# Edits to the opening and the ending of a convolution kernel: warm-up, order of the transposes, one operand made by VectorE, release of the weight loads, and the last tile's second half on ScalarE

## Chip, cores, metric

One NeuronCore of one Trainium2 chip. The metric is device microseconds of one execution. A profile's span is 1.8 us shorter than the time of the execution that it was taken from.

## The reference, cut to what matters

```python
B, T, D, K = 2, 4000, 512, 5          # bf16
xp = jnp.pad(x, ((0,0),(2,2),(0,0)))
h = sum(xp[:, i:i+T, :] @ w1[i] for i in range(5))   # convolution of 5 taps
h = gelu(h)[:, ::2, :]                               # stride 2
f = gelu(conv5(h, w2))[:, ::2, :]                    # the same again, stride 2
j = tanh((f @ w_f)[:, :, None] + (g @ w_g)[:, None]) # U = 8
return j @ w_o                                       # (2, 1000, 8, 512)
```

(`sum` and `conv5` stand for the loops of the original.)

## The kernel before

x is kept transposed (channels on partitions) and split into four phases, the time index modulo 4. Four products of a tap weight with a phase can be saved by making combined operands, called a0, a1, a2, a3, b1, b2, b3 (a0 is phase 2 one step back, minus phase 2). The very first tile, t0 (254 columns), must start before any of this is ready. So half of its output blocks are computed directly, tap by tap (`direct(i)`: 16 matmuls with tap i), and the other half from the combined operands (`filt("a0")`: 8 matmuls with tap 0, and so on). The second tile, t1, and all later ones use the combined operands alone.

The opening, in the program's order:

```python
NWARM = 8
memset(zero[:])                        # on POOL
...
act(warm[0:1], warm[1:2], ACT.Gelu_apprx_tanh)
xr_in = [load_xr(rt) for rt in range(2)]          # two blocks of x, 512 KB each, not transposed

def load_w1(i, after=None):
    o = load_w("sp", w1_sb[i], ...)               # tap i: 512 KB
    if after is not None:
        o.deps[("dma", after.idx)] = True         # issued only when `after` has landed

load_w1(0)
for i in (1, 3, 4, 2):
    load_w1(i, xr_in[1])
for ph in (2, 3, 1, 0):
    load_x(0, ph, 272, 528)                       # transposing DMA: the rest of x
...
warm_mm(NWARM)                                    # the warm-up: matmuls on zeros
for rt in range(2):                               # block of x
    for pp in range(2):                           # 0: even phases, 1: odd phases
        ...                                       # 8 transposes on PE, then a copy out of PSUM:
        if pp: act(o, pv, ACT.Copy)               # odd phases by ScalarE
        else:  ... tensor_copy                    # even phases by VectorE
    warm_mm(1 + rt)
...
for w in ("a0", "b1", "a3"):
    t0.shift(w)                                   # ScalarE copies a phase, moved by one column
for w in ("a1", "a2", "b3", "a0", "b1", "a3"):
    t0.xf(w)                                      # VectorE adds or subtracts
...
for i in (0, 1, 3):
    direct(i)
filt("a0", "b1")
direct(4)
filt("b3", "a3")
direct(2)
...
for w in ("a0", "b1", "a3"):
    t1.shift(w)                                   # a3 waits for the last phase of x
...
filt("b2", "a1", "a2")
for m in (0, 1):
    t0.gelu(m, ps.pair(m * NT, 256, NA))          # ScalarE; frees PSUM banks 0 and 1, where t1 starts
```

All loads are issued by SyncE, in order. A release that has not come holds every load behind it as well: in the profile of before SyncE waited 3.2 us for the second block of x and issued no load between 1.63 and 5.30. The ending evicts the last tile in two halves, both on VectorE, and stores both from SyncE.

Of the kernel before, what the change touches and what calls it, by code (L numbers as in the profile page):

```python
# [201 lines left out]
def bass_standalone__seq2seq_rnn_t_joint__speech_kernel(  # L202
# [30 lines left out]
    NSLOT = 12  # L233
    BU = B * U
    NT = 512
    NWARM = 8

    with ExitStack() as es:  # L238
        cur = [16512]

        def at(name, shape, dtype, offset=None):
            o = cur[0] if offset is None else offset
            b = Buf(nc, name, shape, dtype, o)
            if offset is None:
                cur[0] = (b.end + 31) // 32 * 32
            return b
# [21 lines left out]
        zero = at("zero", [NT], BF16)  # L268
# [11 lines left out]
        pl = Plan(nc)  # L280
        sub, add = ALU.subtract, ALU.add

        def memset(v):
            pl.op("pool", lambda e: e.memset(v.ap, 0.0), (), (v,))

        def tt(eng, o, a, b, op):
            pl.op(eng, lambda e: e.tensor_tensor(out=o.ap, in0=a.ap, in1=b.ap, op=op), (a, b), (o,))  # L287

        def act(o, i, func, scale=1.0, bias=None):
            rd = (i,) if bias is None else (i, bias)  # L290
            pl.op("act", lambda e: e.activation(o.ap, i.ap, func, scale=scale,  # L291
                                                bias=0.0 if bias is None else bias.ap), rd, (o,))

        def mm(o, pairs, start, stop, check=True):

            def fn(e):
                for n, (l, r) in enumerate(pairs):
                    ins = e.matmul(o.ap, lhsT=l.ap, rhs=r.ap, start=start and n == 0,  # L298
                                   stop=stop and n == len(pairs) - 1, skip_group_check=not check)
                return ins  # L300
            pl.op("pe", fn, [v for pr in pairs for v in pr], (o,))


        memset(zero[:])
        memset(warm[:])
        idv = ident[:]
        pl.op("pool", lambda e: e.affine_select(
# [7 lines left out]
        def load_w(eng, dst, src):  # L315
            return pl.dma(eng, lambda e: e.dma_start(dst.ap, src), (), (dst,))

        def load_xr(rt):
            dst = xr[rt][:].map(lambda a: a.rearrange("p r k c -> p (r k c)"))
            src = x[0, 4 * P * rt:4 * P * (rt + 1), :].rearrange("(p r) c -> p (r c)", r=4)  # L320
            return pl.dma("sp", lambda e: e.dma_start(dst.ap, src), (), (dst,))  # L321

        def load_x(s, ph, lo, hi):
# [5 lines left out]
            src = x[b, 4 * i0 + ph:4 * (i0 + hi - lo - 1) + ph + 1:4, :]  # L329
            pl.dma("sp", lambda e: e.dma_start_transpose(out=dst.ap, in_=src), (), (dst,))  # L330

        act(warm[0:1], warm[1:2], ACT.Gelu_apprx_tanh)
        xr_in = [load_xr(rt) for rt in range(2)]

        def load_w1(i, after=None):
            o = load_w("sp", w1_sb[i], w1[i].rearrange("(k c) d -> c k d", c=P))
            if after is not None:
                o.deps[("dma", after.idx)] = True

        load_w1(0)  # L340
        for i in (1, 3, 4, 2):
            load_w1(i, xr_in[1])
        for ph in (2, 3, 1, 0):
            load_x(0, ph, 272, 528)
        for ph in (2, 3, 1, 0):
# [4 lines left out]
        def warm_mm(n):  # L350
            o, z, zz = ps.cols(3 * NT, NT), zero[0:P], zero[:]
            for _ in range(n):
                mm(o, [(z, zz)], True, True)

        warm_mm(NWARM)
        psb = ps.h[:, :].bitcast(BF16)
        for rt in range(2):
            for pp in range(2):
                bk = 4 + 2 * pp + rt
                pv = View(psb[:, bk * 1024:(bk + 1) * 1024].rearrange("p (r k c) -> p r k c", r=2, k=NK), np.array([bk]), True)  # L360

                def fn(e, rt=rt, pp=pp, pv=pv):
                    for r in range(2):
                        for k in range(NK):
                            ins = e.transpose(pv.ap[:, r, k, :], xr[rt].h[:, 2 * r + pp, k, :], ident.h[:, :])
                    return ins
                pl.op("pe", fn, (xr[rt][:], ident[:]), (pv,))
                o = xs[0][pp::2, :, 16 + rt * P:16 + (rt + 1) * P]
                if pp:
                    act(o, pv, ACT.Copy)  # L370
                else:
                    pl.op("dve", lambda e, o=o, pv=pv: e.tensor_copy(out=o.ap, in_=pv.ap), (pv,), (o,))
            warm_mm(1 + rt)


        def shift(src, off, dst, c0, n, which):
# [4 lines left out]
        def xf(src, off, dst, c0, n, which, keep=False):  # L381


            ph = lambda r: src[r, :, off:off + n]
            o = lambda kind: dst[kind, :, c0:c0 + n]
            h = NT // 2
            if which == "b3" and keep:
                tt("dve", dst[0, :, h:h + n], ph(3), ph(1), sub)
            elif which == "a2" and keep:
                tt("dve", dst[1, :, h:h + n], ph(2), ph(0), sub)  # L390
            elif which == "a0":
                tt("dve", o(0), o(0), ph(2), sub)
            elif which == "a3":
                tt("dve", o(2), o(2), ph(0), sub)
            elif which == "b1":
                tt("dve", o(3), o(3), ph(1), sub)
            elif which == "b3":
                tt("dve", ph(3), ph(3), ph(1), sub)
            elif which == "a1":
                tt("dve", o(1), ph(0), ph(2), add)  # L400
            elif which == "a2":
                tt("dve", ph(2), ph(2), ph(0), sub)
# [141 lines left out]
        def direct(i):  # L544
            for m in (0, 1):
                for s in range(2):
                    r, d = tap_at[i][s]
                    mm(ps.cols(m * NT + 256 * s, NA),
                       [(w1_sb[i, k, m * P:(m + 1) * P], xs[0][r, k, 16 + d:16 + d + NA]) for k in range(NK)],
                       i == 0 and s == 0, i == 2, False)  # L550
# [3 lines left out]
        def filt(*which):  # L554
            for w in which:
                for m, A in base0.items():
                    C = A + NT
                    o = {"a0": A, "b1": A, "b3": A + 256, "a3": A + 256, "b2": C, "a1": C, "a2": C + 256}[w]
                    t0.product(w, m, o, w in ("a0", "b2"))

        for w in ("a0", "b1", "a3"):
            t0.shift(w)
        for w in ("a1", "a2", "b3", "a0", "b1", "a3"):
            t0.xf(w)
        wsum13(w1_sb, w1_t, "dve")
        w1sums(1, "s")
        for i in (0, 1, 3):
            direct(i)
        filt("a0", "b1")
        direct(4)  # L570
        filt("b3", "a3")
        direct(2)
# [61 lines left out]
        def tanh(v, k):  # L634

            b, u = v // U, v % U
            lo, hi = v * T2, (v + 1) * T2
            while lo < hi:
                n = min(hi - lo, RING - lo % RING)
                t = lo - v * T2  # L640
                act(jT[k, lo % RING:lo % RING + n], feT[b][k, t:t + n], ACT.Tanh,
                    bias=geT[k * BU + v:k * BU + v + 1])
                lo += n
# [36 lines left out]
        slot_sem = [[nc.alloc_semaphore(f"s_o{i}"), 0] for i in range(NSLOT)]  # L680
        pend = []
        for jt in range(ntile):
            if jt == 4:
                fe(1)
            c0 = jt * P
            while not pend and done < B * U and done * T2 < c0 + P + 900:
                pend = [(done, k) for k in range(NK)]
                done += 1
            while pend and pend[0][0] * T2 < c0 + P:
                tanh(*pend.pop(0))  # L690
            if pend:
                tanh(*pend.pop(0))
            r0, s = c0 % RING, jt % NSLOT
            last = jt == ntile - 1
            for h in range(2 if last else 1):
                w = NT // 2 if last else NT
                cl = slice(h * w, (h + 1) * w)
                v = ps.cols(bank(), w)
                mm(v, [(jT[k, r0:r0 + P], wo_sb[k, cl]) for k in range(NK)], True, True)
                o = ost[s][cl]  # L700
                if jt % 6 == 5 and not last:
                    act(o, v, ACT.Copy)
                else:
                    pl.op("dve", lambda e, o=o, v=v: e.tensor_copy(out=o.ap, in_=v.ap), (v,), (o,))  # L704
                lo = c0
                while lo < c0 + P:
                    vv = lo // T2
                    n = min((vv + 1) * T2, c0 + P) - lo
                    b, u, t = vv // U, vv % U, lo % T2
                    src = ost[s].rows(lo - c0, lo - c0 + n, cl)  # L710
                    dst = out[b, t:t + n, u, cl]
                    pl.dma("sp", lambda e, src=src, dst=dst: e.dma_start(dst, src.ap), (src,), (), slot_sem[s])
                    lo += n

        pl.emit(block, [(s[0], s[1]) for s in slot_sem])
# [28 lines left out]
```

## Time and profile before

| | before |
|---|---|
| time, median of the 3 runs | 279.28 us (279.26 to 279.63) |
| time of the profiled execution | 280.62 us |
| its span | 278.8 us |
| PE busy | 273.8 us (98%) |

From the page of the kernel before: the span, the first lines of the busy times, and the chain that ended last (the work followed back from the last instruction; shares of the span).

```profile
span 278.8 us, 3866 instructions
...
PE 273.8 (98%) x1435; PEld 138.8 (50%) x1435; DVE 188.1 (67%) x243; ACT 163.2 (59%) x193; POOL 30.9 (11%) x39
...
PE acc L298 95%; DMA w_sb<-in_w_dram 2%; DMA xr_64<-in_x_dram 1%; DVE ost_85 L704 0%; SPq L321 0%; DVEq L238 0%; DVE ost_84 L704 0%
```

The same chain in order of time, kernel before (start, length in us, what):

```profile
1.17 4.11 DMA xr_64<-in_x_dram
5.28 0.02 issue
5.30 5.44 DMA w_sb<-in_w_dram
10.74 0.05 issue
10.78 264.00 PE acc L298 x1368
274.78 0.02 issue
```

The second block of x lands at 5.28; that releases the tap-1 weights, which land at 10.74; from there PE works for 264.00 us without a break. The timeline of PE, kernel before (start, length, what; in brackets the idle time ahead and what ended it):

```profile
1.30 3.59 PE L298 MATMUL acc<-zero 128*128 128x512 bf16 x8 [1.30 <-POOL warm L284]
4.68 1.91 PE L365 MATMUL acc<-ident,xr_63 128*128 128x128 bf16 x16
6.39 0.63 PE L298 MATMUL acc<-zero 128*128 128x512 bf16 x1
6.82 1.11 PE L365 MATMUL acc<-ident,xr_64 128*128 128x128 bf16 x16
7.76 0.59 PE L298 MATMUL acc<-zero 128*128 128x512 bf16 x2
8.31 1.90 PE L298 MATMUL acc<-xs_49,w_sb 128*128 128x254 bf16 x16
10.78 3.65 PE L298 MATMUL acc<-xs_49,w_sb 128*128 128x254 bf16 x32 [0.57 <-DMA w_sb<-in_w_dram]
```

Warm-ups, transposes of the two blocks (16 in 1.7 us, one every 107 ns, then 16 in 0.9, one every 56 ns behind the first: by the trace's clock record the clock turned full at 6.92, as the second block began), fillers, `direct(0)` from 8.31. Then 0.57 us of idle time until tap 1 lands; `direct(1)` and `direct(3)` follow in one piece. This is the only place where PE waits after 1.3 us.

### The profile page before, as it was taken

How to read it: one execution, taken by the hardware profiler on the slowest of the kernel's cores; microseconds unless marked ns; L12 is line 12 of the kernel's file. 1: busy time of each engine (PE TensorE's matmuls, PEld its weight loads, DVE VectorE, ACT ScalarE, POOL GpSimd, SP SyncE). 2: the span in 40 equal slices, each digit the busy share in tenths (PEclk: the TensorE clock that was granted, in tenths of full speed). 3: DMA queues.
4: the chain of work that ended last, by engine and by line, in shares of the span. 5: the costliest groups of instructions: out<-in, count | busy, mean ns of one | idle time of the engine just before them, and what ended most of it. 6: DMA issues, size and time to landing. Idle time of an engine off the chain costs nothing.

```text
span 278.8 us, 3866 instructions
## 1 busy us (share of the span) xinstructions
PE 273.8 (98%) x1435; PEld 138.8 (50%) x1435; DVE 188.1 (67%) x243; ACT 163.2 (59%) x193; POOL 30.9 (11%) x39
## 2 busy tenths in 40 slices
PE   8999999999999999999999999999999999999995
PEld 4799954444444444444444444444444444444442
DVE  0899979866997676685434364776665766766764
ACT  2659738338327633822346475948957957966930
POOL 1000000079995000000000000000000000000000
PEclk9999999999999999999999999999999999999999
DMA  6999999992000000000000020444444445444444
GB/s 232 308 158 228 206 207 172 286 314 84 0 0 0 2 0 0 0 2 0 0 2 0 1 75 21 151 151 153 153 153 160 149 145 168 144 153 155 145 150 139
DMA packets 54719, 31.85 MB, mean 114 GB/s; under 512 B 31646, under 2 KB 54446, under 8 KB 54702
## 3 DMA queue, kind: packets, MB, share of 16 engines
q1 hardware_dynamic: 54702, 31.62, 42.4%
q8 instruction: 11, 0.18, 0.3%
q14 instruction: 6, 0.05, 0.1%
HBM read 7.86 MB, written 16.38 MB: 87 GB/s over the span
## 4 chain that ended last, share of the span: by engine, by line
PE 95%; DMA 3%; issue 0%; DVE 0%; SPq 0%; DVEq 0%
PE acc L298 95%; DMA w_sb<-in_w_dram 2%; DMA xr_64<-in_x_dram 1%; DVE ost_85 L704 0%; SPq L321 0%; DVEq L238 0%; DVE ost_84 L704 0%
## 5 line engine op out<-in xcount | busy, mean ns | idle before, releaser
L298 PE MATMUL acc<-wo_sb,jT 128*128 128x512 bf16 (+1 forms) x504 | 108.3, 377 | 0.0
L298 PEld LDWEIGHTS acc<-wo_sb,jT 128*128 128x128 bf16 x504 | 49.3, 98 | 58.8
L298 PE MATMUL acc<-xt_55,w_sb 128*128 128x500 bf16 (+1 forms) x192 | 42.1, 357 | 0.0
L291 ACT ACTIVATE jT<-feT_79,geT 128x1000 bf16<-128x1000 f32 (+6 forms) x44 | 35.8, 889 | 0.0
L291 ACT ACTIVATE jT<-feT_78,geT 128x1000 bf16<-128x1000 f32 (+4 forms) x40 | 35.1, 948 | 0.0
L298 PE MATMUL acc<-xt_54,w_sb 128*128 128x500 bf16 (+1 forms) x160 | 33.2, 342 | 0.0
L298 PEld LDWEIGHTS acc<-xt_55,w_sb 128*128 128x128 bf16 x192 | 18.8, 98 | 18.2
L291 ACT ACTIVATE cs_65<-acc 128x500 f32<-128x500 f32 (+2 forms) x13 | 7.0, 539 | 32.2 <-PE acc L298 32.2
L298 PEld LDWEIGHTS acc<-xt_54,w_sb 128*128 128x128 bf16 x160 | 15.6, 98 | 13.1
L291 ACT ACTIVATE cs_66<-acc 128x500 f32<-128x500 f32 (+2 forms) x13 | 7.0, 537 | 22.5 <-PE acc L298 22.5
L298 PE MATMUL acc<-xs_49,w_sb 128*128 128x254 bf16 (+2 forms) x112 | 15.7, 286 | 0.6 <-DMA w_sb<-in_w_dram 0.6
L291 ACT ACTIVATE ost_92<-acc 128x512 bf16<-128x512 f32 x10 | 6.0, 597 | 16.4 <-PE acc L298 16.4
L704 DVE CAST ost_81<-acc 128x512 bf16<-128x512 f32 x11 | 7.6, 691 | 10.4 <-PE acc L298 10.4
L704 DVE CAST ost_87<-acc 128x512 bf16<-128x512 f32 x10 | 6.9, 692 | 10.3 <-PE acc L298 10.3
L298 PE MATMUL acc<-xs_49,w_t 128*128 128x246 bf16 (+2 forms) x72 | 13.8, 315 | 0.0
L287 DVE TENSOR_TENSOR ty_68<-ty_68,acc 128x1000 f32<-128x1000 f32 (+2 forms) x9 | 9.7, 1077 | 5.2 <-PE acc L298 5.2
L287 DVE TENSOR_TENSOR ty_67<-ty_67,acc 128x1000 f32<-128x1000 f32 (+2 forms) x9 | 9.7, 1077 | 5.1 <-PE acc L298 5.1
L298 PEld LDWEIGHTS acc<-xs_49,w_sb 128*128 128x128 bf16 x112 | 10.7, 97 | 4.1 <-DMA w_sb<-in_w_dram 0.8
L291 ACT ACTIVATE ost_86<-acc 128x512 bf16<-128x512 f32 x10 | 5.9, 593 | 11.4 <-PE acc L298 11.4
L287 DVE TENSOR_TENSOR ty_69<-ty_69,acc 128x1000 f32<-128x1000 f32 (+1 forms) x8 | 8.5, 1061 | 3.5 <-PE acc L298 3.3
L298 PE MATMUL acc<-xt_55,w_t 128*128 128x500 bf16 (+1 forms) x48 | 10.0, 340 | 0.0
L704 DVE CAST ost_85<-acc 128x512 bf16<-128x512 f32 (+1 forms) x12 | 7.7, 646 | 2.6 <-PE acc L298 2.6
(113 smaller groups left out, 368.4 us busy)
## 6 DMA issues: line engine op xcount, KB each, us to landing
w_sb<-in_w_dram SPq DMA_DIRECT2D x10, 512.0 KB, 6.7
out_dram<-ost_81 SPq DMA_DIRECT2D x11, 128.0 KB, 1.9
out_dram<-ost_83 SPq DMA_DIRECT2D x10, 128.0 KB, 1.9
out_dram<-ost_85 SPq DMA_DIRECT2D x10, 128.0 KB, 1.9
out_dram<-ost_89 SPq DMA_DIRECT2D x10, 128.0 KB, 1.9
out_dram<-ost_82 SPq DMA_DIRECT2D x9, 128.0 KB
out_dram<-ost_84 SPq DMA_DIRECT2D x9, 128.0 KB
out_dram<-ost_86 SPq DMA_DIRECT2D x9, 128.0 KB
```

The source lines that it names most:

```text
L287: pl.op(eng, lambda e: e.tensor_tensor(out=o.ap, in0=a.ap, in1=b.ap, op=op), (a, b), (o,))
L291: pl.op("act", lambda e: e.activation(o.ap, i.ap, func, scale=scale, bias=0.0 if bias is None else bias.ap), rd, (o,))
L298: ins = e.matmul(o.ap, lhsT=l.ap, rhs=r.ap, start=start and n == 0, stop=stop and n == len(pairs) - 1, skip_group_check=not check)
L704: pl.op("dve", lambda e, o=o, v=v: e.tensor_copy(out=o.ap, in_=v.ap), (v,), (o,))
```

## The change

The intent: fill PE's wait for tap 1 with work that needs tap 0 alone. a0 needs only the even phases, so these are turned first, VectorE makes a0 in one subtraction from the phase itself (read one column back, so not aligned to 4 bytes) without ScalarE's copy, and its products go right behind `direct(0)`. A longer warm-up without fillers, started earlier by a zero fill on VectorE instead of POOL, is meant to have the clock full before the transposes, which in the profile of before began 2.2 us ahead of the turn (4.69 and 6.92). The release of tap 3 is moved from the landing of the second x block to that of tap 0 (tap 4 and tap 2 stand behind it in the same queue), so that until then only tap 1 is queued behind tap 0. The second half of the last tile goes to ScalarE and its queue. The core of the diff, with cuts:

```diff
-    NWARM = 8
+    NWARM = 10
...
-        memset(zero[:])
+        pl.op("dve", lambda e: e.memset(zv.ap, 0.0), (), (zv,))
...
-        load_w1(0)
-        for i in (1, 3, 4, 2):
-            load_w1(i, xr_in[1])
+        came.append(load_w1(0))          # came = [x block 0, x block 1, tap 0]
+        for i, after in ((1, came[1]), (3, came[2]), (4, None), (2, None)):
+            load_w1(i, after)
...
-        for rt in range(2):
-            for pp in range(2):
+        for pp in range(2):
+            for rt in range(2):
...
-            warm_mm(1 + rt)
...
+            if which == "a0" and keep:
+                tt("dve", o(0), src[2, :, off - 1:off - 1 + n], ph(2), sub)
...
-        for w in ("a0", "b1", "a3"):
+        for w in ("b1", "a3"):
             t0.shift(w)
-        for w in ("a1", "a2", "b3", "a0", "b1", "a3"):
+        for w in ("a0", "a1", "a2", "b3", "b1", "a3"):
             t0.xf(w)
...
-        for i in (0, 1, 3):
-            direct(i)
-        filt("a0", "b1")
+        direct(0)
+        filt("a0")
+        direct(1)
+        direct(3)
+        filt("b1")
...
-                if jt % 6 == 5 and not last:
+                if h == 1 or jt % 6 == 5 and not last:
...
-                    pl.dma("sp", lambda e, ...
+                    pl.dma(("sp", "act")[h], lambda e, ...
```

More of the change, by code (lines that the diff above doesn't have):

```diff
@@ L301, in mm @@
             pl.op("pe", fn, [v for pr in pairs for v in pr], (o,))
-        memset(zero[:])
+        zv = zero[:]
+        pl.op("dve", lambda e: e.memset(zv.ap, 0.0), (), (zv,))
         memset(warm[:])
@@ L330, in load_x @@
             pl.dma("sp", lambda e: e.dma_start_transpose(out=dst.ap, in_=src), (), (dst,))
+        came = [load_xr(rt) for rt in range(2)]
         act(warm[0:1], warm[1:2], ACT.Gelu_apprx_tanh)
-        xr_in = [load_xr(rt) for rt in range(2)]
         def load_w1(i, after=None):
@@ L338, in load_w1 @@
                 o.deps[("dma", after.idx)] = True
-        load_w1(0)
-        for i in (1, 3, 4, 2):
-            load_w1(i, xr_in[1])
+            return o
+        came.append(load_w1(0))
+        for i, after in ((1, came[1]), (3, came[2]), (4, None), (2, None)):
+            load_w1(i, after)
         for ph in (2, 3, 1, 0):
@@ L386, in xf @@
             h = NT // 2
-            if which == "b3" and keep:
+            if which == "a0" and keep:
+                tt("dve", o(0), src[2, :, off - 1:off - 1 + n], ph(2), sub)
+            elif which == "b3" and keep:
                 tt("dve", dst[0, :, h:h + n], ph(3), ph(1), sub)
@@ L711, in bass_standalone__seq2seq_rnn_t_joint__speech_kernel @@
                     dst = out[b, t:t + n, u, cl]
-                    pl.dma("sp", lambda e, src=src, dst=dst: e.dma_start(dst, src.ap), (src,), (), slot_sem[s])
+                    pl.dma(("sp", "act")[h], lambda e, src=src, dst=dst: e.dma_start(dst, src.ap), (src,), (), slot_sem[s])
                     lo += n
```

## The prediction

> **What bounds it now.** TensorE. PE is busy 273.8 of 278.8 us (page), and the chain of waits is one PE piece from 10.78 to 274.78. So only the first 10.8 us and the last 4 can give time. The chain of the opening: load of the second x block (lands 5.29) -> its landing releases the issue of the tap-1 weights (5.30) -> these land at 10.74 -> PE. Before that, the timeline shows 8 warm-ups at 427 ns from 1.30, 16 transposes at 107 ns (4.69 to 6.39), then the second block at 56 ns: the granted clock went full at 6.92. Tap 0 runs 8.31 to 10.05; PE then waits 0.6 us for tap 1. The tail: the last two half evictions share VectorE (0.41 us each), their two stores share one queue (issues end 276.34 and 276.83, last landing 278.10), then 0.7 us of closing.
>
> **What the change moves.**
> - Zero fill on VectorE instead of POOL (0.53 us): warm-up starts about 0.3 us earlier, at 1.0; ten warm-ups then end near 5.25, where the second block is there (5.29).
> - Even phases first: 16 transposes, then the second VectorE copy ends near 7.9 if the clock turns at 6.9 as before (7.1 if it turns by 5). Tap 0 starts at 7.7 to 8.0 (tap-0 weights land 7.62).
> - Operand a0 is one VectorE subtraction, no ScalarE copy (1.04 us).[...] I expect 0.69 us as for aligned ones[...].
> - Its 8 products (109 ns each = 0.87 us) run behind tap 0 and fill PE's wait for tap 1: the main gain.
> - Tap-3 weights now wait for tap 0's landing (7.6 instead of 5.72). Tap 1 then lands earlier (estimate 9.3 to 10.5), tap 3 near 12.5 (before 12.41[...]), and the x phases behind it 0.3 to 0.6 later.
>
> **On the critical path.** Tap 1 starts near 10.6 with a0 done: 1.1 us ahead of before. Some is lost: tap 3 may be waited for; the second tile cannot start before the first tile's gelu (21.97 to 22.56), which stands on ScalarE behind the copy of the last x phase (landed 21.02). That caps the gain at 23.81 - 22.60 = 1.2 us less the delay of that phase. Head: 0.75 us gained. Tail: the second half goes to ScalarE and its queue, about 0.25 us.
>
> **Predicted: 278.3 us, range 277.6 to 279.1.** Faster by over 2%: 1%; within 2%: 98%; slower: 1%.
>
> **What would show it.** Right: one PE block from about 7.9, a0 products directly behind tap 0; PE's last matmul 0.7 earlier; last landing 0.25 nearer to it. Wrong: PE waits for tap-3 weights over 0.5 us; a0 over 1.2 us and PE waiting on VectorE; a PE gap near 22 to 24 on gelu or late x phases.
>
> **What would make it wrong.** The clock turning late:[...] before turned 2.2 us after transposes began, so I keep 6.9. Turning at 8 costs about 0.5 us. Delaying x by over 1 us would take the head's gain away.

279.28 less 0.75 for the head and 0.25 for the tail is 278.28, the 278.3 given. The 0.69 us for a0 is the time of the aligned subtractions in the profile of before (0.680 to 0.689). The 0.5 us for a turn at 8 is an estimate from that profile: 1.1 us more at 107 instead of 56 ns for a transpose, of which about half is lost.

## The result

| | before | after |
|---|---|---|
| median of 6 executions, same rounds | 279.41 us (279.26 to 279.94) | 280.59 us (279.46 to 281.10) |
| time of the profiled execution | 280.62 us | 279.65 us |
| span of its profile | 278.8 us | 277.8 us |

The ratio is 1.003, with a 95% interval from 1.0008 to 1.0053: slightly slower, though at the 2% mark this and every other run here counts as the same. Ratios here are the mean time of one kernel's fast runs over that of the other's of the same rounds, so they are not quite the ratio of the medians that I quote. The predicted 278.3 us, and even the range up to 279.1, lie below every execution of the changed kernel. Luck has a part in the size of the loss: none of these six executions of before was a slow one, where 22 of 61 are over all rounds (below). Over all rounds the means are 280.48 and 280.00 us.

The profiles say the opposite of the times: 1.0 us *faster*. The profile of before comes from an unusually slow execution of before, and that of after from one of the two fastest of after. The six times of after are 279.46, 279.65, 280.58, 280.60, 280.64 and 281.10.

The page of the changed kernel:

```profile
span 277.8 us, 3862 instructions
...
PE 272.7 (98%) x1434; PEld 137.7 (50%) x1434; DVE 187.4 (67%) x243; ACT 162.5 (58%) x193; POOL 30.7 (11%) x38
...
PE acc L298 91%; SPq L331 3%; DMA w_sb<-in_w_dram 2%; DMA xs<-in_x_dram 2%; SPq L317 0%; ACT xt L291 0%; SPq L322 0%; ACT hT L291 0%; ACT ost L291 0%
```

The chain in order of time, changed kernel, cut:

```profile
1.63 5.46 DMA w_sb<-in_w_dram
7.09 0.02 issue
7.11 0.37 SPq L317
...
17.12 4.21 DMA xs<-in_x_dram
21.33 0.02 issue
21.35 1.02 ACT xt L291
22.37 0.50 ACT hT L291
22.87 0.05 issue
22.92 251.86 PE acc L298 x1256
```

PE is the limit for 91% now, not 95%. The part shown starts with tap 0, whose landing at 7.09 releases the next load. It goes on through the queue of loads to the last phase of x (21.33), through ScalarE's copy of it and the gelu behind that copy, to the start of t1 at 22.92. So there is a second limit, in the chain of loads, that before did not show. PE's timeline, changed kernel:

```profile
1.17 3.95 PE L298 MATMUL acc<-zero 128*128 128x512 bf16 x10 [1.17 <-DVE zero L305]
4.96 1.95 PE L367 MATMUL acc<-ident,xr 128*128 128x128 bf16 x32
7.14 1.92 PE L298 MATMUL acc<-xs,w_sb 128*128 128x254 bf16 x16 [0.23 <-DMA w_sb<-in_w_dram]
8.89 1.03 PE L298 MATMUL acc<-xt,w_sb 128*128 128x254 bf16 x8
9.76 1.91 PE L298 MATMUL acc<-xs,w_sb 128*128 128x254 bf16 x16
12.11 1.91 PE L298 MATMUL acc<-xs,w_sb 128*128 128x254 bf16 x16 [0.44 <-DMA w_sb<-in_w_dram]
```

The eight products of a0 stand at 8.89, right behind `direct(0)`, as intended, and `direct(1)` follows without a wait. Then PE waits for tap 3 (0.44 us). a0 itself: VectorE's timeline has the four unaligned and aligned subtractions in one line for after, and the three aligned ones for before.

```profile
6.93 2.48 DVE L287 TENSOR_TENSOR xt<-xs 128x1016 bf16<-128x1016 bf16 x4
```

```profile
8.24 1.88 DVE L287 TENSOR_TENSOR xt_55<-xs_49 128x1016 bf16<-128x1016 bf16 x3
```

The first of the four, from 6.93 on, is a0. By its own record it took 0.691 us, the others 0.678 to 0.681; the first of the aligned three in before took 0.686. Being unaligned cost next to nothing.

### The profile page after: what moved, and what is told of

Same layout as the page of the kernel before. It is cut to its first block, busy times and chain, and to the rows that moved or that the text cites. A ratio compares the mean times of both kernels' runs of the same rounds, so it can differ in the third digit from the quotient of the medians.

```text
span 277.8 us, 3862 instructions
## 1 busy us (share of the span) xinstructions
PE 272.7 (98%) x1434; PEld 137.7 (50%) x1434; DVE 187.4 (67%) x243; ACT 162.5 (58%) x193; POOL 30.7 (11%) x38
## 4 chain that ended last, share of the span: by engine, by line
PE 91%; SPq 4%; DMA 3%; ACT 1%; issue 0%
PE acc L298 91%; SPq L331 3%; DMA w_sb<-in_w_dram 2%; DMA xs<-in_x_dram 2%; SPq L317 0%; ACT xt L291 0%; SPq L322 0%; ACT hT L291 0%; ACT ost L291 0%
## 5 line engine op out<-in xcount | busy, mean ns | idle before, releaser
L709 DVE CAST ost<-acc 128x512 bf16<-128x512 f32 (+1 forms) x105 | 72.2, 689 | 35.6 <-PE acc L298 35.6
L298 PE MATMUL acc<-xt,w_sb 128*128 128x500 bf16 (+2 forms) x352 | 75.3, 350 | 0.2 <-ACT hT L291 0.2
L291 ACT ACTIVATE jT<-feT,geT 128x1000 bf16<-128x1000 f32 (+5 forms) x84 | 70.9, 917 | 0.0
L298 PEld LDWEIGHTS acc<-xt,w_sb 128*128 128x128 bf16 x352 | 34.3, 98 | 31.8 <-ACT hT L291 0.5
L520 DVE SCALAR_TENSOR_TENSOR ty<-acc,cs 128x500 f32<-128x500 f32 (+2 forms) x52 | 29.7, 612 | 22.4 <-PE acc L298 22.1
L287 DVE TENSOR_TENSOR ty<-ty,acc 128x1000 f32<-128x1000 f32 (+2 forms) x26 | 27.9, 1072 | 14.7 <-PE acc L298 14.5
L291 ACT ACTIVATE ost<-acc 128x512 bf16<-128x512 f32 (+1 forms) x21 | 12.3, 585 | 31.5 <-PE acc L298 31.5
L298 PE MATMUL acc<-xs,w_t 128*128 128x500 bf16 (+2 forms) x136 | 29.9, 342 | 0.0
L298 PE MATMUL acc<-xs,w_sb 128*128 128x254 bf16 (+2 forms) x144 | 23.9, 305 | 0.7 <-DMA w_sb<-in_w_dram 0.7
L291 ACT ACTIVATE xt<-xs 128x2000 bf16<-128x2000 bf16 (+2 forms) x14 | 21.5, 1564 | 5.0 <-DMA xs<-in_x_dram 5.0
L291 ACT ACTIVATE hT<-ty 128x1000 bf16<-128x1000 f32 (+2 forms) x18 | 17.4, 965 | 3.2 <-DVE ty L287 3.2
```

The costliest lines, as they stand in the source:

```text
L287: pl.op(eng, lambda e: e.tensor_tensor(out=o.ap, in0=a.ap, in1=b.ap, op=op), (a, b), (o,))
L291: pl.op("act", lambda e: e.activation(o.ap, i.ap, func, scale=scale, bias=0.0 if bias is None else bias.ap), rd, (o,))
L298: ins = e.matmul(o.ap, lhsT=l.ap, rhs=r.ap, start=start and n == 0, stop=stop and n == len(pairs) - 1, skip_group_check=not check)
L520: pl.op("dve", lambda e, o=o, f=f: e.scalar_tensor_tensor(out=o.ap, in0=d.ap, scalar=f, in1=c.ap, op0=ALU.mult, op1=add), (d, c), (o,))
L709: pl.op("dve", lambda e, o=o, v=v: e.tensor_copy(out=o.ap, in_=v.ap), (v,), (o,))
```

## The experiments

"Landing" is when the sixteenth and last DMA engine reports a load: each of these loads has 16 reports in the trace's semaphore records, which I take as one for each of the 16 engines of the page. "Group" means a cluster of the times of one kernel. Over all rounds the kernel before had 61 executions, not counting before_again and before_look: 31 under 279.8 us, 22 at 280.2 or more, 8 between, mean 280.00. The changed kernel was run 12 times: mean 280.48. A run has six executions, unless said otherwise, and is compared with those of before on the same chip. Idle times of PE are those of the timeline.

Theory L (loads; the expectations also speak of a release theory and of lagging engines, its two parts): the loads decide, and the new release costs time. Rival C (clock): what separates the executions is when PE's clock turns full; it turned at 6.92 us in the profile of before and at 4.49 in that of after. Rival F (floor): the gelu behind the copy of the last x phase holds t1.

| run | mean | mean of before, same rounds | 95% interval of the ratio | profiled execution |
|---|---|---|---|---|
| before_again | 280.01 | 279.85 | 0.998 to 1.003 | 280.76 |
| after_again | 280.62 | 279.85 | 0.999 to 1.005 | 281.30 |
| after_old_loads | 279.71 | 279.85 | 0.997 to 1.002 | 279.80 |
| before_new_loads | 280.44 | 279.85 | 1.000 to 1.005 | 280.03 |
| tail_only | 280.27 | 280.19 | 0.998 to 1.002 | 280.33 |
| after_no_release | 280.03 | 280.19 | 0.997 to 1.002 | 281.11 |
| old_loads_late_a0 | 280.63 | 280.19 | 0.998 to 1.005 | 280.51 |
| old_loads_gelu_first | 279.23 | 280.19 | 0.994 to 0.999 | 279.57 |
| before_look (2 executions) | 280.81 | 279.81 | 1.000 to 1.007 | 281.35 |
| before_gelu_first | 280.43 | 279.81 | 1.000 to 1.005 | 279.63 |
| after_gelu_first | 280.26 | 279.81 | 0.998 to 1.005 | 280.13 |
| old_loads_no_warmup | 280.10 | 279.81 | 0.999 to 1.003 | 279.15 |
| old_loads_again | 279.54 | 280.31 | 0.995 to 1.000 | 279.17 |
| old_gelu_again | 279.51 | 280.31 | 0.994 to 0.999 | 280.41 |
| early_tap1_gelu_first | 279.21 | 280.31 | 0.994 to 0.999 | 278.99 |
| before_x_held | 279.89 | 280.31 | 0.996 to 1.002 | 279.28 |
| early_tap1 | 279.28 | 280.12 | 0.995 to 0.999 | 279.60 |
| before_early_tap1 | 279.75 | 280.12 | 0.996 to 1.001 | 279.75 |

The 280.31 of one set of rounds and the 279.81 of another are the same kernel: with 11 executions, the share that falls in the slow group decides the mean. That is why a single ratio here says less than the profiles do.

### Both kernels again

No edit.

> The kernel before, unchanged, for a second profile. Its profiled execution took 280.6 us, its six timed ones 279.3 to 279.9, so the profile read for the prediction may show a slower opening than the usual one. Clock theory: the moment the clock turns full differs between executions (6.92 us in that profile) and sets the time; a profile of about 279.4 us has the turn before 5 us and tap 0 starting by 7.6. Load theory: the tap-1 weights land at different times; a profile of about 279.4 us has them by 9.7 instead of 10.74, whatever the clock does. If neither differs and the time does, both fall. Times: 279.3 to 279.9 again.

> The changed kernel, unchanged, for a second profile and more times. Its six times lay in two groups, 279.5 to 279.7 (with the profile: clock full at 4.49) and 280.6 to 281.1. Clock theory: two groups again, and a profile from the slow group has the clock full at 6.5 or later and its 32 transposes mostly at 107 ns, tap 0 starting about 8.5 to 9. Load theory: a profile from the slow group has tap 3 landing at 13 or later with PE waiting over 1 us for it, the clock playing no part.

before_again gave both groups by itself: 279.31, 279.39, 279.41 and 280.59, 280.61, 280.76. Its profile is again from the slow group (280.76): tap 1 landed at 10.88, PE waited for it. after_again's profile is a slow one too, 281.30. Its clock turned at 4.93, about as early as in the fast profile of after (4.49), so rival C is out for this pair. What differs is tap 3, from PE's timeline of after_again:

```profile
7.54 1.92 PE L298 MATMUL acc<-xs,w_sb 128*128 128x254 bf16 x16 [0.41 <-DMA w_sb<-in_w_dram]
9.29 1.03 PE L298 MATMUL acc<-xt,w_sb 128*128 128x254 bf16 x8
10.15 1.91 PE L298 MATMUL acc<-xs,w_sb 128*128 128x254 bf16 x16
13.82 1.36 PE L298 MATMUL acc<-xs,w_sb 128*128 128x254 bf16 x11 [1.76 <-DMA w_sb<-in_w_dram]
```

PE waited 1.76 us for tap 3, which was issued at 7.51 and landed at 13.77. In the fast profile of after it was issued at 7.11 and landed at 12.06. In both, the time is tap 3's landing plus 267.5 or 267.6 us (12.06 and 279.65; 13.77 and 281.30).

The reports of the 16 engines show why it was late. These are the sorted landing times of the engines, in us, from the trace's semaphore records:

```
after_again, tap 3: 10.80 10.81 10.81 11.12 11.14 11.14 11.17 11.18 11.19 11.25 11.31 11.32 11.38 13.26 13.32 13.77
after,       tap 3: 11.34 11.44 11.52 11.56 11.58 11.59 11.59 11.62 11.62 11.63 11.64 11.70 11.73 11.81 11.87 12.06
before,      tap 1:  8.64  8.71  8.77  8.77  8.78  8.82  8.83  8.87  8.91  8.91  8.94  9.01  9.08  9.13 10.55 10.74
```

In the first and the last row two or three engines stand 1.4 to 2.4 us behind the last of the rest, and the load has landed only with the last of them. PE went on only behind the last report: in after_again it started on tap 3 at 13.82 (last report 13.77), in before on tap 1 at 10.78 (10.74).

### The release alone, in both directions

After with the old release, and before with the new one:

```diff
 after_old_loads, old_loads_again:
-        for i, after in ((1, came[1]), (3, came[2]), (4, None), (2, None)):
+        for i, after in ((1, came[1]), (3, came[1]), (4, None), (2, None)):
 before_new_loads:
-        load_w1(0)
-        for i in (1, 3, 4, 2):
-            load_w1(i, xr_in[1])
+        w1_0 = load_w1(0)
+        for i, after in ((1, xr_in[1]), (3, w1_0), (4, None), (2, None)):
+            load_w1(i, after)
```

> The changed kernel with the old release of the tap-3 weights (behind the landing of the second x block, not of tap 0). Clock theory: still two groups about 1.1 us apart, because the transposes still wait on the clock. Load theory: one group, near 279.3 us or below, with tap 1 landing near 10.7 again. If the new order is what costs, the mean falls by 0.5 us or more against the changed kernel.

> The kernel before with only the new release of the tap-3 weights (behind the landing of tap 0). Clock theory: time moves by under 0.3 us, one group as before. Load theory: 0.5 us or more slower than before, or two groups, with PE waiting for tap 3 at about 12 to 13 us.

> The changed kernel with the old release again, for a larger sample: its first six times had a mean of 279.7 beside 279.85 of before. If the release was the whole loss, it stays 0.6 us or more under the changed kernel (12 executions so far: 279.5 to 281.4, mean 280.5), and level with before or up to 0.5 us under it. If its first result was luck of the lagging engines, it moves to 280.3 or more.

The old release brought the changed kernel from a mean of 280.48 (12 executions) to 279.63 (12 executions: 279.71 and 279.54 in the two runs), that is 0.85 us; in the one set of rounds that had both, 280.62 and 279.71. The new release alone moved before up by 0.6 us in its rounds (280.44 against 279.85), but that interval includes 1. I call the cost of the release shown by the first direction, 12 executions against 12; the second agrees in sign and roughly in size, and would not carry it alone. The forecast that both groups would stay 1.1 us apart with the old release (rival C) missed: its twelve times run from 279.15 to 280.26.

Why it costs, shown by the windows (busy time of each engine in a stretch, then clock, DMA share and GB/s). First the changed kernel, then a kernel with the old release in a fast execution (before_x_held, below), both from 8 to 11 us:

```profile
8.00:9.00 1.00, 1.00 (x11) 0.89 (x10) 1.00 (x3) 0.97 (x2) 0.00 (x0) 1.00 1.33 256
9.00:10.00 1.00, 1.00 (x12) 0.90 (x10) 0.86 (x2) 1.00 (x2) 0.00 (x0) 1.00 0.39 73
10.00:11.00 1.00, 1.00 (x12) 0.90 (x10) 0.75 (x2) 0.46 (x1) 0.00 (x0) 1.00 1.07 372
```

```profile
8.00:9.00 1.00, 1.00 (x11) 0.90 (x10) 1.00 (x3) 1.00 (x3) 0.00 (x0) 1.00 1.07 371
9.00:10.00 1.00, 0.84 (x8) 0.51 (x7) 0.83 (x3) 1.00 (x2) 0.00 (x0) 1.00 1.07 373
10.00:11.00 1.00, 1.00 (x12) 0.89 (x10) 0.75 (x2) 0.88 (x1) 0.00 (x0) 1.00 1.10 372
```

With the new release the DMA engines move 73 GB/s between 9 and 10 us, where they move 373 with the old one. In this microsecond the four profiles with the new release show 73 to 190 GB/s, the sixteen others 318 to 379. Tap 1 has passed through, and tap 3, issued at 7.11 to 7.48, is hardly moving yet. Without a lagging engine, tap 3 lands at 11.0 to 11.2 with the old release (before_x_held: 10.99, old_loads_again: 11.17, old_loads_no_warmup: 11.21) and at 11.9 to 12.1 with the new one (before_new_loads: 11.89, after: 12.06). What stands behind it in the queue is late as well, down to the phases of x (the last one at 21.33 in after, at 19.68 and 20.11 in the two fast profiles of before's opening). What the new release buys is real but worth less: tap 1 landed at 9.2 to 9.8 in all four profiles with it, and at 10.2 to 11.5 in eight of the twelve that kept the old one.

### What the two groups of before are

> The kernel before, for a profile of a fast execution (about 279.3 us). In ten profiles so far PE needs 251.56 us from the start of the second tile (t1) to its last matmul, so the time is t1's start plus 256.8. A fast one must start t1 at 22.4 to 22.6, against 23.8 to 24.0 in the two slow profiles. Floor theory: t1 then waits for the gelu behind the copy of the last x phase (gap of 0.1 us or more there), tap 1 has landed by 9.7. Rival, no floor: PE runs through from tap 0 to t1 with no gap. If this profile is slow again (280.6), it only repeats what is known.

> The kernel before with the first transposing x load held until tap 1 has landed. If it is the preparation of the transposing loads (issued from 7.4) that makes engines lag in tap 1, its 16 landings lie within 0.7 us of each other (8.7 to 9.4) and the slow group of times disappears: all within 279.2 to 279.6. If not, tap 1 lands as late as 10.5 or later in about half of the executions, and the two groups stay, 0 to 0.3 us slower.

before_look (no edit, for a profile) was slow again: tap 1 at 11.46, time 281.35. before_x_held holds the first transposing load until tap 1 has landed:

```diff
         for ph in (2, 3, 1, 0):
-            load_x(0, ph, 272, 528)
+            o = load_x(0, ph, 272, 528)
+            if ph == 2:
+                o.deps[("dma", held[0].idx)] = True     # held[0] is tap 1
```

Its times still show both groups (279.21 to 279.79, and 280.72, 280.81), so the transposing loads behind tap 1 do not seem to make the engines lag (the slow executions have no profile); that rival missed. But its profile is what I had lacked, a fast execution of the opening of before. All that the edit does ahead of tap 1's landing is to keep SyncE from issuing that one load at 7.4. Its chain in order of time:

```profile
5.26 4.14 DMA w_sb<-in_w_dram
9.40 0.04 issue
9.45 264.00 PE acc L298 x1368
```

This is the same chain as in before, and the same 264.00 us, but it starts at 9.45 instead of 10.78. The 1.33 us are the whole difference (1.34) between the profile that I predicted from (280.62) and the median that I subtracted from (279.28). PE's only wait for weights in this execution:

```profile
PE acc L298 <- DMA w_sb<-in_w_dram: 0.2, 1, 0.2
```

The relation holds throughout: in all five profiles of before's opening with its own ending and release, the time is tap 1's landing plus 269.9 us (10.74 and 280.62; 10.88 and 280.76; 11.46 and 281.35; 9.72 and 279.63; 9.41 and 279.28). In these five the slow ones are those in which engines lagged in tap 1; that the executions without a profile divide in the same way is inferred. In the same five the clock also turned late in the slow ones (6.35 to 6.92 us) and early in the fast ones (4.32 and 4.99), so rival C seems to fit. But PE stood waiting for tap 1 in all five (0.57, 0.99 and 1.32 us in the slow ones, 0.77 and 0.16 in the fast ones), so an earlier clock would only have lengthened the wait.

### a0's place

```diff
 old_loads_late_a0, against after_old_loads:
-        direct(0)
-        filt("a0")
-        direct(1)
-        direct(3)
-        filt("b1")
+        for i in (0, 1, 3):
+            direct(i)
+        filt("a0", "b1")
```

> The changed kernel with the old release and with a0's products back behind tap 3. If a0's products fill the wait for tap 1, only executions with a late tap 1 (10.7 to 10.9) suffer: the slow group goes from about 279.9 (changed kernel with the old release) to 280.6 or more, the fast group stays near 279.2. If a0's place is worth nothing, the groups stay at 279.2 and 279.9.

As forecast, its fast executions stayed (279.27, 279.65) and the slow ones went up: 280.51, 280.51, 280.91, and one of 282.95, against at most 280.26 among the twelve with a0 in the new place. Its profile (of an execution of 280.51) has tap 1 at 10.77 and PE idle for 1.01 us behind `direct(0)`. The profiled execution of after_old_loads, with tap 1 as late (10.92), took 279.80. PE's next line in the two, a0 late first:

```profile
10.81 3.65 PE L298 MATMUL acc<-xs,w_sb 128*128 128x254 bf16 x32 [1.01 <-DMA w_sb<-in_w_dram]
```

```profile
10.97 3.65 PE L298 MATMUL acc<-xs,w_sb 128*128 128x254 bf16 x32 [0.56 <-DMA w_sb<-in_w_dram]
```

Counted from tap 1's landing, the time is 269.74 us with a0 late and 268.88 with a0 in its new place. The difference, 0.86 us, is that of the eight products (0.87). So the intended gain exists in the executions where tap 1 is late; in the two fast ones no gain can be seen. The 282.95 is unexplained.

### No release, and the first block as release

```diff
 after_no_release:
+        for i, after in ((1, None), (3, None), (4, None), (2, None)):
 early_tap1, early_tap1_gelu_first (after with it); before_early_tap1 (before with the same two releases):
+        for i, after in ((1, came[0]), (3, came[1]), (4, None), (2, None)):
```

> The changed kernel with no release at all on the weight loads: all issued in a row. Release theory (a load that is held until another has landed leaves its engines without packets[...]): tap 1 lands near 8.0 and tap 3 near 9.5 on most engines, PE waits for neither, mean 279.4 or below, 0.9 us or more under the changed kernel. Lagging-engine theory (one to three of the 16 engines fall about 1.5 us behind in some executions, whatever the order): there are still two groups about 0.5 to 1.3 us apart. Rival, that the release protects the x blocks: the second x block lands later than 5.4 and tap 0 starts after 8.5, no gain.

The trace of after shows a rate under 200 GB/s from 8.5 to 10.0 us (189, 70, 25, 29, 78 and 160 GB/s in quarters of a microsecond), between tap 1 and tap 3.

> The gelu-first version with tap 1 released by the first x block (about 4.0) and tap 3 and the rest by the second (about 5.3), so that the engines are never without packets. Release theory: tap 1 lands by 8.6 on most engines, tap 3 by 10.2, all x phases about 0.7 earlier, mean at least 0.3 under the old release; 278.5 to 279.2. Lagging-engine theory: with more loads queued behind one another the lag comes earlier or oftener (as in the version with no release, where tap 0 landed at 9.58), and the mean is no better: 279.5 or more.

> The changed kernel with tap 1 released by the first x block and tap 3 by the second, the gelus where the change has them. The same with the gelus first stood at 279.0 to 279.4 with no slow group. If the release is the whole matter: 279.0 to 279.6, at least 0.9 us under the changed kernel's mean of 280.5. If the gelu order was needed for it (late x phases, a gap at 22 to 23), the mean rises to 279.6 or more.

> The kernel before with only tap 1 released by the first x block instead of the second. In before the time is the landing of tap 1 plus 269.9 us, in two groups (9.4 and 10.6 to 11.5). If tap 1 lands at 8.5 to 9.0, before is bound by tap 0 and its own matmuls instead: 279.0 to 279.6 without a slow group, level with early_tap1, and the rest of the change is then worth under 0.3 us. If a0's place and the turning order matter, early_tap1 is 0.3 us or more faster than this one. If lagging engines strike tap 1 here too, the slow group stays.

Without any release, two groups stayed (279.21 to 279.56, and 280.45 to 281.11). In its profile it was tap 0 that had lagging engines: it landed at 9.58, with the fastest engine at 6.42, and `direct(0)` began at 9.63. The second x block landed at 5.35, no later than elsewhere, so the release does not protect x as the rival had it. But the mean forecast (279.4 or below) missed.

Releasing tap 1 by the *first* x block (landed at about 4.0) and tap 3 by the second gave the kernels that beat both, before and after. early_tap1 had all times within 278.84 to 279.66, a mean of 279.28, and a ratio of 0.997 (0.995 to 0.999); with the gelus first 278.99 to 279.41, 279.21 and 0.996 (0.994 to 0.999). There is no slow group, although engines lagged here too: tap 3 landed at 11.58 in the latter's profile, with its fastest engine at 9.31. In these two profiles tap 1 lands at 8.53 and 9.40 and tap 3 at 11.58 and 11.18, and PE comes for tap 3 at about 11.9 and 12.5 only (40 matmuls of 109 ns behind the start of tap 0 at 7.55 and 8.11). So in these two a lag of one load no longer reached PE. The chain of early_tap1 (page) is PE nearly from the start:

```profile
PE 98%; issue 0%; ACT 0%; DVE 0%
PE acc L298 97%; PE acc L367 1%; ACT ost L291 0%; DVE zero L305 0%
```

The same releases in before gave 279.75 (279.14 to 280.19), also without the slow group at 280.6. My expectation left two outcomes open, level times or 0.3 us and more between the two; early_tap1 is 0.47 us faster in the same rounds. So the rest of the change is worth about half a microsecond once the loads are released well. With six executions each this is an estimate, not a measured split. The changed kernel with the old release, 0.45 us under before in its two sets of rounds (279.63 against 280.08), agrees.

### The floor: the gelu behind the copy

```diff
-        for w in ("a0", "b1", "a3"):
+        for w in ("a0", "b1"):
             t1.shift(w)
...
+        for m in (0, 1):
+            t0.gelu(m, ps.pair(m * NT, 256, NA))
+        t1.shift("a3")
         for w in ("a1", "a2", "a3"):
             t1.xf(w)
         filt("b2", "a1", "a2")
-        for m in (0, 1):
-            t0.gelu(m, ps.pair(m * NT, 256, NA))
```

> The changed kernel with the old release, and the first tile's two gelus put on ScalarE ahead of the copy that waits for the last x phase. Cap theory: in fast executions the second tile waits for a gelu that stands behind that copy (PE gap of 0.5 us at 22.4 in the changed kernel's profile), so the fast group gains 0.3 to 0.7 us: 278.5 to 278.9; the slow group (PE there late anyway) gains under 0.2. If the cap plays no part, both groups stay at 279.2 and 279.9.

> The kernel before with only the gelus moved ahead of the copy that waits for the last x phase. Floor theory: the fast group falls below 279.2 (278.6 to 279.1), the slow group stays at 280.6 to 280.9. Rival, no floor in before: both groups as they were. Mean 0 to 0.4 us under before.

> The changed kernel, new release kept, with the gelus moved ahead. The release costs by itself: PE still waits for tap 3 (0.4 to 1.9 us), so the mean stays above that of the same kernel with the old release (279.2) by 0.6 us or more; the floor taken away is worth 0.3 to 0.5 against the changed kernel: 280.0 us on the mean. If the release cost only by pushing the x phases (the floor) back, it falls to 279.3.

> The changed kernel with the old release and the gelus first, again: 279.2 beside 280.2 of before at first. If the gelu order is worth something, this stays at least 0.3 us under the one with the old release alone in these rounds; if its first result was luck, the two are level.

On the old release it looked like a gain at first (279.23), but next to the same kernel without it, in the same rounds, it is level (279.51 and 279.54; on the early release 279.21 and 279.28 in different rounds). On before it gained nothing (280.43 against 279.81 in its rounds, three of six executions slow). The fast profile of old_loads_again shows why: the last x phase lands at 19.95, the gelu is done at 21.48, and t1 starts at 22.49 straight behind PE's other work. The floor does not bind there. Rival F falls for before. Only the profiles of after and after_again have PE idle ahead of t1, for 0.23 and 0.20 us, with the last x phase at 21.33 and 23.01; before_new_loads, with the same release, has none. What moving the gelus away is worth in after_gelu_first stays open: its mean of 280.26 contains one unexplained execution of 282.70, and the other five average 279.77, beside 279.63 with the old release in other rounds. Its profile (280.13) has t1 starting at 22.61, but then 0.79 us of small gaps inside t1, whose last phase of x came at 22.42.

### Warm-up and ending

```diff
 old_loads_no_warmup, against after_old_loads:
-    NWARM = 10
+    NWARM = 0
 tail_only: before with the last two edits of the change
```

> The changed kernel with the old release and no warm-up matmuls at all: PE's first work is at 4.0[...]. Clock theory (what separates the groups is when the clock turns): all executions at 281 us or more. Load theory: the transposes end near 8 instead of 6.9, tap 0 runs partly at half rate, and 1 to 2 us are lost where tap 1 comes early, 0.3 to 1 where it comes late: 280.2 to 281 us. If the time is unchanged (279.7), the warm-up is worth nothing here.

> The kernel before with only the new ending (second half of the last tile evicted by ScalarE and stored from its queue). My estimate from the trace of before was 0.25 us of gain; the changed kernel's profile had 3.35 us from the start of the last matmul to the end, before 3.45, which says 0.1. A profile shows 3.2 to 3.4 us; the times move by 0.1 to 0.25 us inside each of the two groups of before (279.3 and 280.7), which the interval will hardly show.

Without any warm-up the changed kernel with the old release took 280.10 against 279.63 with it in other rounds: 0.5 us on the mean, where rival C asked for 281 in every execution. Its profiled execution, 279.15, had no lagging engine and was as fast as the best with the warm-up, although the clock turned only at 7.46, the latest of all profiles, with 32 transposes from 4.06 on as PE's only work until then. Rival C is out as what separates the groups. The ending: in the profiles of tail_only, after and early_tap1 the end comes 3.33 to 3.35 us after the start of the last matmul, in before 3.45. That is 0.1 us, below what the times can show. The second store's issue ends 0.36 us earlier relative to the last matmul (1.10 instead of 1.46), but the last landing is only 0.10 earlier (2.63 instead of 2.73).

## Why the prediction was wrong, point by point

Two steps failed. The 1.0 us of gain was subtracted from a median of three fast executions (279.28), although it had been read from a slow one (280.62): an error of 1.3 us. Subtracted from that execution's own time it gives 279.6, which is what the two fastest executions of after took (279.46 and 279.65). And the new release of tap 3, booked together with the gelu's limit as a loss of about 0.35 us ("1.1 us ahead", "0.75 us gained"), measured 0.85 us, more than the half microsecond that the rest of the change is worth. By these figures that made the change a loss.

- **"PE's wait for tap 1 is filled with a0's products: the main gain."** The mechanism is right. The first failed step is the baseline. The wait was read from a profile of 280.62 us and the gain subtracted from a median of 279.28. The wait of 0.57 us belongs to that execution, with its late tap 1 (10.74). In a fast execution of nearly the same opening (before_x_held) tap 1 lands at 9.41 and PE waits 0.16. The other fast profile, before_gelu_first, has a wait of 0.77, because tap 0 had started at 7.08 there: what is to be filled differs between executions. The warning was in the data that I had: the profiled execution was 1.0 us slower than the slowest timed one (279.63).
- **"Tap-3 weights now wait for tap 0's landing … tap 3 near 12.5 (before 12.41)"; "Some is lost".** The landing was near the forecast in the fast profile (12.06) and 1.3 us later in the slow one (13.77). But it was compared with the slow execution's 12.41, where it looks free. Where no engine lags, tap 3 lands at 11.0 to 11.2 with the old release and 11.9 to 12.1 with the new one. I had PE arriving for it at 12.3; in the fast profile of after it arrived at 11.67, because tap 0 had started at 7.14 and not at 7.7 to 8.0. This is the second failed step, the term that I booked as a small loss. The profiles of after show it as PE's wait for tap 3: 0.44 and 1.76 us.
- **"The second tile cannot start before the first tile's gelu … caps the gain."** Seen in both profiles of after (0.23 and 0.20 us), with x phases that the new release made late. The forecast delay of 0.3 to 0.6 us holds only against the slow profile (21.33 against 21.02). In the two fast profiles of before's opening the last phase lands at 19.68 and 20.11, so it is over 1 us late, and that is what the prediction named as taking the head's gain away. The limit does not bind with the old release.
- **Head 0.75 us.** Between the two profiles, PE's last matmul did come 0.88 us earlier (275.37 to 274.49) and the span fell by 1.0, as summed. Comparing two single profiles would have confirmed a forecast that the times refute.
- **Tail 0.25 us.** Measured 0.1: the landing did not follow the earlier issue.
- **a0 on VectorE at 0.69 us.** Right: 0.691, where the aligned ones in the same profile took 0.678 to 0.681.
- **Clock.** The prediction kept 6.9 for its moment. Over the 18 profiles in which the turn is recorded it came at 4.3 to 7.5. With warm-ups that all began at 1.2 to 1.3 it still ranged from 4.3 to 7.1, and what sets it was not shown. It did not separate the two groups. Once no load bound PE it may count: early_tap1's profile (turn at 7.10, tap 0 from 8.11) took 279.60, that of early_tap1_gelu_first (5.61, 7.55) 278.99. Tap 0 also landed late in the first (8.05), so this is not shown.
- **Range and chances.** "Within 2%" held. The range (277.6 to 279.1) took no account of the two groups of before, more than 1 us apart, although a time of 280.62 beside 279.28 was in the data.

What stays open: why an engine falls behind in one execution and not in another. The trace does not tell which engine a packet belongs to. It was struck in tap 0 (after_no_release), tap 1 (before) and tap 3 (after_again). Holding back the transposing loads did not remove the slow executions.

## What to carry to other kernels

Before a wait read from a profile is booked as a gain, compare the time of the profiled execution with the timed ones. If they differ by more than the gain hoped for, the wait may belong to that execution alone. When the order of loads is tuned, look at the landing of all 16 engines, not only at the last: here a load that was held until another had *landed* left the DMA engines with little to move (73 GB/s for a microsecond in after), and it hung on the slowest engine of the load before it (in after tap 0's last report came at 7.09, the one ahead of it at 6.93, and tap 3 was issued at 7.11). Release loads early enough that a lag of one load stays in front of the compute engine; here that took the slow group away (12 executions, none above 279.66), where filling the wait with other work only narrowed it (279.15 to 280.26).
